# A gated mix of linear attention and a gated MLP on one core: attention's banks copied out whole and stored by rows, its products placed later, one chunk of an operand asked for later

## The chip, the cores and the metric

The kernel runs on one core of one Trainium2 chip. The metric is the device time of one execution in microseconds. The core has five engines that run side by side: PE (matrix products, TensorE), DVE (VectorE), ACT (ScalarE), POOL (GpSimd) and SP (SyncE). In this kernel SP issues the loads and POOL the stores; both go to the same 16 DMA engines.

## The reference

For 2048 tokens of 1024 values, a linear attention with 32 heads and learned feature maps, and a gated MLP, are mixed by a gate per token:

```python
g = sigmoid((x * gate_w).sum(-1, keepdims=True))
q, k, v = split(x @ wqkv)                                  # 32 heads of 32
phi_q = concat(softmax(q @ w_phi), softmax(-(q @ w_phi)))  # phi_k likewise
kv, z = phi_k^T v, sum(phi_k)
a = concat_heads((phi_q kv) / (phi_q z + 1e-6)) @ wo
b = (gelu(x @ w_gate) * (x @ w_up)) @ w_down               # 1024 -> 3584 -> 1024
out = g * a + (1 - g) * b
```

## The kernel before, in words

**Products.** Each large product is split in two by rows, columns and depth, and is made of seven half-size products of sums in place of eight (Strassen's scheme). Each factor is written as a high and a low part in the type fp32r (`high`, a copy on ACT at line 56; `low`, a subtraction on DVE at line 59), and three passes, high by high, high by low and low by high, make one product: 12 matmuls of 128x512 for a depth of 512.

**Units.** The first stage runs over 80 units, in four groups: values, keys, and the two halves of the tokens with queries, gate and up columns. The change from one group to the next is called a change; the third is the one to the last group. A unit has seven slots, in each of which PE makes one of the seven products: a<-x10, p<-s1, c<-x01 (of the unit before), a<-s2, a<-s4 (of the unit before), c11<-x11, b<-s3. The names a, b, c, c11 and p are PSUM banks; x10, s1, s2, x11, s3, s4 and x01 are the seven sums of the token side, each with parts h and l, each read in four chunks of 512. Operands of the weight side live in `wgu`, `tyz` (three buffers) and `v`. At a change the seven token-side sums are loaded anew in chunks to a home, and split; PLANS lists for each change which sum is asked for at which slot and where (line 515). For the last change the home "g" has three places, so the fourth chunk of s4 waits until the first has been split, is then loaded to its place (line 535), and is waited for by `change_parts` (lines 520 to 538).

**Work beside PE.** What ACT, DVE and SP do in a slot is decided while the program is built: each piece of work is a generator that yields the slot from which it may go, the slot by which it must, and its cost on DVE and on ACT, and `run_slot` puts those that fit into the slot. A list called `fillers` holds small products that are put between two of the seven; an entry gives the time from which it may stand. The scheduler knows no loads and no stores: what an engine waits for on the chip is not in its costs. Each engine then runs its own instructions strictly in the order that was written.

**Attention.** In the last group 32 jobs of attention run beside the units. A job loads queries, forms exponentials on ACT (line 1127), normalizes on DVE (1150 to 1173), transposes (1181), splits into high and low (`split_weights`, on lines 56 and 59 into `pts`), and lets PE make four matmuls of 128x512 into two banks called `misc` (line 1198, `attend`). `both` (line 1183) takes the two banks out: the product's halves stand crosswise in the two banks, and their sum is stored to `la` in HBM by a store and an accumulating store. The hidden tiles `h` (three buffers, in turn) hold what goes to HBM: two per job, and those of the units with up columns (DVE lines 760, `less`, and 707), which are stored to `lm`. `h<-b` on line 760 is DVE's subtraction at a unit's start, behind which ACT copies b into c (line 779), into which PE's c<-x01 adds two products later.

**Opening.** Units 1 and 2 also carry out what prepares the first sums; a table called `extra` lists it by slot. `step(1)` is the last of four subtractions (line 149) of raw tiles that stand in `tyz`'s buffers.

**The last stage** multiplies the stored `la` and `lm` by `wo` and `w_down` (line 1462) and adds into the result.

Of the kernel before, what the change touches and what calls it, by code (L numbers as in the profile page):

```python
# [10 lines left out]
AF = mybir.ActivationFunctionType  # L11
OP = mybir.AluOpType
# [21 lines left out]
def tile_gated_mix(ctx: ExitStack, tc: tile.TileContext, x, xT, wkT, wqT, wv, w_phi, wo,  # L34
                   w_gate, w_up, w_down, gate_w, out):
    nc = tc.nc
# [18 lines left out]
    def high(dst, src):  # L55
        nc.scalar.activation(dst, src, AF.Copy)  # L56

    def low(dst, src, dst_h):
        nc.vector.tensor_tensor(dst, src, dst_h.bitcast(F32), OP.subtract)  # L59
# [17 lines left out]
    def hidden():  # L77
        return fa.tile([P, BLK], F32, tag="h", name="h", bufs=3)
# [3 lines left out]
    def x_part(i, part, dtype=F32R):  # L82
        pool = ring if i % 3 == 0 else xa if i < 3 else fa
        return pool.tile([P, KC // 2, BLK], dtype, name=X_NAMES[i] + "hl"[part], bufs=1)
# [24 lines left out]
    left_att = [[dram.tile([2, 2, P, 2, BLK], F32, name=f"la{h}{d}") for d in range(N_ATT)] for h in range(2)]  # L109
# [21 lines left out]
    def spill(h, dst, j, m, **how):  # L131

        nc.gpsimd.dma_start(dst[m // 4][j, m % 2, :, m // 2 % 2, :], h, **how)  # L133
# [52 lines left out]
    with tc.manual_schedule(engines={PE, DVE, ACT, SP}):  # L186
# [30 lines left out]
        for s in range(KC):  # L217
            kc, i = kcs[s], s // 2
# [25 lines left out]
        for s in range(KC):  # L244
            kc, i = kcs[s], s // 2
# [14 lines left out]
            for n, (a, e) in enumerate(PASSES):  # L260
                for blk in (1, 0):
                    for f in range(2):
                        nc.tensor.matmul(plain_banks[blk, f], wide_w[a][:, kc, f * P:(f + 1) * P], xq[blk][e],
                                         start=s == 0 and n == 0, stop=s == KC - 1 and n == 2)
# [25 lines left out]
        def sum_parts(k, q):  # L290
            src, *dst = [t[:, 2 * q:2 * q + 2] for t in (whole[SUM_AT[k]], *x_ops[0, (1, 2, 4, 5)[k]])]
            return (lambda: high(dst[0], src)), (lambda: low(dst[1], src, dst[0]))
# [17 lines left out]
        def sums_high(k, *qs):  # L310
            if x_ops[0, (1, 2, 4, 5)[k]][0] is None:
                x_ops[0, 5] = [x_part(5, part) for part in range(2)]
            for q in qs:
                sum_parts(k, q)[0]()

        def sums_low(k, *qs):
            for q in qs:
                sum_parts(k, q)[1]()
# [14 lines left out]
        streams, fillers, now = [], [], [0]  # L333
        clock, tensor = [0.0, 0.0], [0.0]

        def start(gen, ready=0.0):
            streams.append([next(gen), len(streams), gen, ready])
# [50 lines left out]
        passed = [0.0]  # L388
# [73 lines left out]
        def change_half(t, half):  # L462

            yield t - 13, NEVER, 0.0
            while keys_left[0]:
                yield now[0] + 1, NEVER, 0.0
            if half == 1:
                plain = lambda j, k: wk_fold[j][4 * k:4 * k + 4].rearrange("k p n -> p k n")
                s4 = k_sum
            else:  # L470
                plain = lambda j, k: xT3[:, 4 * k:4 * k + 4, (2 * HALF[half] + j) * BLK:(2 * HALF[half] + j + 1) * BLK]
                s4 = x_sum[HALF[half]]
            srcs = [plain(1, 0), s4[0], s4[1], plain(1, 1), s4[2], s4[3], plain(0, 1)]
            homes = {}
            for i, at, home in PLANS[half]:
                yield t + at, t + at, 0.0
                while home in busy or half == 2 and (gating[0] if home in ("w", "y") else folding[0]):
                    yield now[0] + 1, now[0] + 1, 0.0
                if isinstance(home, int):
                    x = x_part(home, 1, F32)  # L480
                    x = [x[:, j] for j in range(KC // 2)]
                else:
                    if home not in homes:
                        homes[home] = home_parts(half, home)
                    x = homes[home]
                busy[home] = KC // 2
                for j in range(len(x)):
                    nc.sync.dma_start(x[j], srcs[i][:, j])
                need = t + (min(NEED[i], NEED[home] - 1) if isinstance(home, int) else NEED[i])
                start(change_parts(half, i, home, x, t, need, srcs[i]))  # L490
# [6 lines left out]
        def home_parts(half, home):  # L497
# [10 lines left out]
            if home == "y":  # L508
# [5 lines left out]
        held_homes, gating = [], [True]  # L514
        PLANS = {1: ((0, -9, "x"), (1, -8, "w"), (2, -5, "x"), (3, -4, "w"), (4, -1, "x"), (6, 1, "w"), (5, 3, "x")),
                 2: ((0, -9, "w"), (1, -8, "y"), (2, -5, "w"), (3, -5, "x"), (4, -4, "y"), (6, 0, "w"), (5, 3, "x")),
                 3: ((0, -7, "x"), (1, -5, "y"), (2, -4, "x"), (3, -3, "z"), (4, -1, 3), (5, 0, "g"), (6, 3, "z"))}

        def change_parts(half, i, home, raw, t, need, src):

            yield max(now[0] + 3, t + LAST[i] + 1), need - 3, 0.0
            while i in busy:
                yield now[0] + 1, now[0] + 1, 0.0
            x_ops[half, i] = [x_part(i, part) for part in range(2)]
            for j in range(KC // 2):
                h = x_ops[half, i][0][:, j]
                if j == 3 and raw[3] is raw[0]:
                    yield now[0] + 3, need - 2, 0.0
                yield now[0], need - 3, 0.0, 0.63
                high(h, raw[j])  # L530
                low_j = low_part(x_ops[half, i][1][:, j], raw[j], h, need, home, j)
                if len(raw) == 3 and not j:
                    yield from low_j
                    raw = [*raw, raw[0]]
                    nc.sync.dma_start(raw[3], src[:, 3])
                else:
                    start(low_j, passed[0])

        def low_part(dst, x, h, need, home, j):

            yield now[0], need - 2, 0.69
            low(dst, x, h)
            busy[home] -= 1
            if not busy[home]:
                del busy[home]
                if home == "z":
                    for k in held_homes:
                        held[k] = False
# [558 lines left out]
        def attention(jobs):  # L1107
# [4 lines left out]
            while job:  # L1112
                half, g, j = job
# [21 lines left out]
                z = shared["z"]  # L1135
# [47 lines left out]
                def both(po, half=half, g=g, j=j):  # L1183
                    yield now[0] + 1, now[0] + 3, 0.0, 1.2
                    hs = [hidden() for _ in range(2)]
                    for i, (a, b) in enumerate(((0, 64), (64, 0))):
                        nc.scalar.activation(hs[i][:64], po[0][a:a + 64], AF.Copy)
                        nc.scalar.activation(hs[i][64:], po[1][b:b + 64], AF.Copy)
                        if i == 0:
                            yield now[0], now[0] + 2, 0.0, 1.2  # L1190
                    spill(hs[0], left_att[half], j, g)
                    spill(hs[1], left_att[half], j, g, accum_op=OP.add)

                def attend(kbs=kbs, pts=pts, both=both):
                    po = [misc(), misc()]
                    for q in range(2):
                        for p in range(2):
                            nc.tensor.matmul(po[p], kbs[:, p].rearrange("p i a b -> p (i a b)"), pts[:, q, p, :],  # L1198
                                             start=q == 0, stop=q == 1)
                    free[0] = True  # L1200
                    start(both(po))

                def push(attend=attend):
                    yield now[0], NEVER, 0.0
                    fillers.append((passed[0], attend, 4, range(1, 7)))

                def split_weights(pts=pts, push=push):
                    yield now[0], NEVER, 0.0, 1.05
                    high(pts[:, 0], f2)
                    yield now[0], NEVER, 1.25  # L1210
                    low(pts[:, 1], f2, pts[:, 0])
                    lows[0] = True
                    start(push())

                start(split_weights(), passed[0])
            while not free[0]:
                yield now[0] + 1, NEVER, 0.0
# [45 lines left out]
        def step(q):  # L1263
            return (lambda: next(x_sums[q])), 1.22
# [4 lines left out]
                    outs[1], (lambda: sums_high(1, 0, 1), 0.0, 2.1), (lambda: sums_low(1, 0, 1), 2.44)],  # L1269
                2: [*folds[2:4], (lambda: sums_high(2, 0, 1), 0.0, 2.1), (lambda: sums_low(2, 0, 1), 2.44), step(0)],  # L1270
                4: [*folds[4:], outs[2], outs[3]]},
            2: {2: [step(1), (lambda: sums_high(3, 0), 0.0, 1.05)],
                3: [(lambda: sums_low(3, 0), 1.22), (lambda: sums_high(3, 1), 0.0, 1.05), (lambda: sums_low(3, 1), 1.22), *puts[:1]],
                5: puts[1:2]},
            3: {1: puts[2:3], 2: puts[3:]}}
        for n, u in enumerate(units):
# [10 lines left out]
    po = [ctx.enter_context(tc.tile_pool(name=f"po{n}", bufs=b, space=PSUM, reuse_waits="tile"))  # L1287
          for n, b in enumerate((3, 3, 1, 1))]
    fours = [[po[n]] * 3 + [po[n + 2]] for n in range(2)]
    with tc.tile_pool(name="op", bufs=1, reuse_waits="tile") as op, tc.manual_schedule(engines={PE, DVE, ACT, SP}):  # L1290
# [142 lines left out]
        for s, (turn, d, k) in enumerate(steps):  # L1433
# [26 lines left out]
            for m, c in order:  # L1460
                for n, (a, e) in enumerate(PASSES):
                    nc.tensor.matmul(ps[c], lefts[s][:, a, m, c * P:(c + 1) * P], made[k][:, e, m],  # L1462
                                     start=d == 0 and m == 0 and n == 0, stop=d == n_duo - 1 and m == 1 and n == 2)
# [40 lines left out]
```

## Time and profile before

| what | us |
|---|---|
| median of three runs (2322.46, 2326.59, 2326.56) | 2326.56 |
| the profiled execution | 2325.13 |
| its span, first to last instruction | 2323.2 |
| PE busy | 2310.4 |
| DVE, ACT, POOL busy | 1746.4, 1206.0, 389.4 |

The span is what the profile's views are about; 1.9 us lie around it. The view of waits says for each engine what it was idle for. In a timeline a row has its start, its duration, the engine, the line, what it writes and reads, how many instructions it merges, and in brackets the idle time before it with what ended it. A matmul's own duration is longer than the distance to the next, since matmuls overlap. `w` is the name of both work tiles.

### The profile page before, as it was taken

How to read it: one execution, taken by the hardware profiler on the slowest of the kernel's cores; microseconds unless marked ns; L12 is line 12 of the kernel's file. 1: busy time of each engine (PE TensorE's matmuls, PEld its weight loads, DVE VectorE, ACT ScalarE, POOL GpSimd, SP SyncE). 2: the span in 40 equal slices, each digit the busy share in tenths (PEclk: the TensorE clock that was granted, in tenths of full speed). 3: DMA queues.
4: the chain of work that ended last, by engine and by line, in shares of the span. 5: the costliest groups of instructions: out<-in, count | busy, mean ns of one | idle time of the engine just before them, and what ended most of it. 6: DMA issues, size and time to landing. Idle time of an engine off the chain costs nothing. (4 is left out here: it accounts for less than half of the span.)

```text
span 2323.2 us, 29698 instructions
## 1 busy us (share of the span) xinstructions
PE 2310.4 (99%) x10414; PEld 1918.5 (83%) x10414; DVE 1746.4 (75%) x2390; ACT 1206.0 (52%) x1691; POOL 389.4 (17%) x620
## 2 busy tenths in 40 slices
PE   9999999999999999999999999999999999999999
PEld 8888888888888888878887888788888888888887
DVE  8677567788888888867888888884774868867874
ACT  6555456565656565546687777775533322323221
POOL 2443322222222222221111111111000000000000
PEclk9999999999999999999999999999999999999999
DMA  7899989888889999997888887787874867977873
GB/s 234 293 324 326 310 301 348 293 310 291 311 298 304 328 311 324 305 319 258 259 261 251 263 255 257 238 258 234 313 245 149 289 236 264 339 253 274 295 262 134
DMA packets 264981, 645.44 MB, mean 278 GB/s; under 512 B 32208, under 2 KB 68576, under 8 KB 256896
## 3 DMA queue, kind: packets, MB, share of 16 engines
q1 hardware_dynamic: 205888, 428.67, 55.3%
q0 software_dynamic: 58672, 214.74, 26.5%
q8 instruction: 82, 1.34, 0.2%
q14 instruction: 67, 0.55, 0.1%
q10 hardware_dynamic: 272, 0.13, 0.0%
HBM read 429.00 MB, written 214.70 MB: 277 GB/s over the span
## 5 line engine op out<-in xcount | busy, mean ns | idle before, releaser
L1462 PE MATMUL po<-tw,wgu 128*128 128x512 f32 x1344 | 309.8, 389 | 0.0
L56 ACT ACTIVATE wgu<-stage 128x1024 fp32r<-128x1024 f32 (+2 forms) x166 | 172.6, 1040 | 255.1 <-DVE stage L1352 159.0
L1462 PEld LDWEIGHTS po<-tw,wgu 128*128 128x128 f32 x1344 | 252.3, 188 | 52.4
L59 DVE TENSOR_TENSOR wgu<-stage,wgu 128x1024 fp32r<-128x1024 f32 (+2 forms) x135 | 161.6, 1197 | 86.8 <-ACT wgu L56 85.8
L747 PE MATMUL a<-s4h,v 128*128 128x512 f32 x632 | 209.1, 392 | 0.0
L747 PE MATMUL c<-x01h,tyz 128*128 128x512 f32 x624 | 205.8, 391 | 1.2 <-ACT c L779 1.2
L747 PE MATMUL p<-s1h,tyz 128*128 128x512 f32 x624 | 205.0, 389 | 1.4 <-ACT w L765 1.4
L747 PE MATMUL a<-s2h,tyz 128*128 128x512 f32 x624 | 205.4, 390 | 0.7 <-DVE tyz L59 0.5
L747 PE MATMUL b<-s3h,tyz 128*128 128x512 f32 x624 | 205.6, 390 | 0.3 <-ACT b L796 0.3
L747 PE MATMUL a<-x10h,wgu 128*128 128x512 f32 x624 | 205.3, 390 | 0.0
L747 PE MATMUL c<-x11h,wgu 128*128 128x512 f32 x624 | 205.0, 389 | 0.0
L1462 PE MATMUL po<-tw,wl 128*128 128x512 f32 x672 | 156.9, 389 | 0.0
L1462 PE MATMUL po<-tyz,wgu 128*128 128x512 f32 x672 | 155.2, 389 | 0.0
L1462 PEld LDWEIGHTS po<-tw,wl 128*128 128x128 f32 x672 | 126.1, 188 | 26.2
L1462 PEld LDWEIGHTS po<-tyz,wgu 128*128 128x128 f32 x672 | 126.1, 188 | 26.2
L747 PEld LDWEIGHTS a<-s4h,v 128*128 128x128 f32 x632 | 119.3, 189 | 24.8
L747 PEld LDWEIGHTS p<-s1h,tyz 128*128 128x128 f32 x624 | 117.1, 188 | 26.7 <-ACT w L765 2.2
L747 PEld LDWEIGHTS c<-x01h,tyz 128*128 128x128 f32 x624 | 117.2, 188 | 25.9 <-ACT c L779 2.1
L747 PEld LDWEIGHTS a<-s2h,tyz 128*128 128x128 f32 x624 | 117.0, 188 | 25.7 <-DVE tyz L59 1.0
L747 PEld LDWEIGHTS b<-s3h,tyz 128*128 128x128 f32 x624 | 117.2, 188 | 24.6 <-ACT b L796 0.7
L747 PEld LDWEIGHTS c<-x11h,wgu 128*128 128x128 f32 x624 | 117.1, 188 | 24.3
L747 PEld LDWEIGHTS a<-x10h,wgu 128*128 128x128 f32 x624 | 117.1, 188 | 24.1
(448 smaller groups left out, 4870.6 us busy)
## 6 DMA issues: line engine op xcount, KB each, us to landing
stage<-lm SPq DMA_DIRECT2D x98, 512.0 KB, 4.4
sr<-in_w_down SPq DMA_DIRECT2D x84, 512.0 KB, 4.9
sl<-lm SPq DMA_DIRECT2D x70, 512.0 KB, 4.7
lm<-h POOLq DMA_DIRECT2D x112, 256.0 KB, 5.2
stage<-in_w_gate SPq DMA_DIRECT2D x42, 512.0 KB, 5.6
stage<-in_w_up SPq DMA_DIRECT2D x42, 512.0 KB, 7.0
vs<-vt SPq DMA_DIRECT2D x32, 512.0 KB, 4.1
la<-h POOLq DMA_DIRECT2D x64, 256.0 KB, 5.0
```

The source lines that it names most:

```text
L56: nc.scalar.activation(dst, src, AF.Copy)
L59: nc.vector.tensor_tensor(dst, src, dst_h.bitcast(F32), OP.subtract)
L747: nc.tensor.matmul(dst, w[:, h, kc, :], xq[e][:, kc, :], start=first and kc == 0 and i == 0, stop=kc == 3 and i == 2, skip_group_check=True)
L1462: nc.tensor.matmul(ps[c], lefts[s][:, a, m, c * P:(c + 1) * P], made[k][:, e, m], start=d == 0 and m == 0 and n == 0, stop=d == n_duo - 1 ...
```

## The change

It has four parts.

1. `both` copies each of the two banks out whole (two ACT copies of 128x512 in place of four of 64x512), and stores by rows: of each tile one half of the rows goes to its place by a plain store, the other half to the other tile's place by an accumulating one, four DMAs of 64x512 in place of two of 128x512. The sums are the same.
2. The attention products may stand 0.8 us later in `fillers`, and the generator that pushes them starts behind the low part of `pts`.
3. At the third change s1 is asked for one slot earlier, and the wait for a fourth chunk is two slots longer and is due one slot later.
4. `step(1)` moves from slot 2 of unit 2 to slot 0.

```diff
-                 3: ((0, -7, "x"), (1, -5, "y"), (2, -4, "x"), (3, -3, "z"), (4, -1, 3), (5, 0, "g"), (6, 3, "z"))}
+                 3: ((0, -7, "x"), (1, -6, "y"), (2, -4, "x"), (3, -3, "z"), (4, -1, 3), (5, 0, "g"), (6, 3, "z"))}
...
                 if j == 3 and raw[3] is raw[0]:
-                    yield now[0] + 3, need - 2, 0.0
+                    yield now[0] + 5, need - 1, 0.0
...
                     hs = [hidden() for _ in range(2)]
-                    for i, (a, b) in enumerate(((0, 64), (64, 0))):
-                        nc.scalar.activation(hs[i][:64], po[0][a:a + 64], AF.Copy)
-                        nc.scalar.activation(hs[i][64:], po[1][b:b + 64], AF.Copy)
-                        if i == 0:
-                            yield now[0], now[0] + 2, 0.0, 1.2
-                    spill(hs[0], left_att[half], j, g)
-                    spill(hs[1], left_att[half], j, g, accum_op=OP.add)
+                    for h, bank in zip(hs, po):
+                        nc.scalar.activation(h, bank, AF.Copy)
+                    dst = left_att[half][g // 4][j, g % 2, :, g // 2 % 2, :]
+                    for i in range(2):
+                        for p in range(2):
+                            nc.gpsimd.dma_start(dst[64 * p:64 * p + 64], hs[p][64 * i:64 * i + 64],
+                                                **(dict(accum_op=OP.add) if i else {}))
...
-                    fillers.append((passed[0], attend, 4, range(1, 7)))
+                    fillers.append((passed[0] + 0.8, attend, 4, range(1, 7)))
...
-                    start(push())
+                    start(push(), passed[0])
...
-            2: {2: [step(1), (lambda: sums_high(3, 0), 0.0, 1.05)],
+            2: {0: [step(1)], 2: [(lambda: sums_high(3, 0), 0.0, 1.05)],
```

On DVE in unit 2 the subtraction of raw tiles (L149) changes places with what follows the copy of b; a piece of the difference, with what goes and what comes:

```order
 L167 TENSOR_TENSOR vh<-c_85,vh 128x4x64 x2
 L760 TENSOR_TENSOR h<-b,w_535 128x512
+L149 TENSOR_TENSOR raw<-raw 128x1024
 L167 TENSOR_TENSOR w_535<-h,w_535 128x4x64 x2
 L59 TENSOR_TENSOR v<-o_646,v 128x512
-L149 TENSOR_TENSOR raw<-raw 128x1024
 L59 TENSOR_TENSOR tyz<-stage,tyz 128x1024
 L59 TENSOR_TENSOR s4l<-raw,s4h 128x1024 x2
```

The subtraction stands two rows, three instructions, earlier.

On ACT behind the third change, in the unit whose s4 is the first of the new half, the order before was (`x01h` and `s4h` are token-side sums, `pts` the exponentials that the sums of keys and values read at line 995):

```order
L56 ACTIVATE x01h<-stage 128x512 x4
L714 ACTIVATE h<-c_85 128x512
L765 ACTIVATE w_535<-p 128x512
L779 ACTIVATE c<-b 128x512
L794 ACTIVATE c_85<-a 128x512
L56 ACTIVATE s4h<-w_535 128x512
L56 ACTIVATE pts<-w_557 128x1024
L56 ACTIVATE wgu<-stage 128x1024
```

and it is now:

```order
L56 ACTIVATE x01h<-stage 128x512 x4
L714 ACTIVATE h<-c_85 128x512
L765 ACTIVATE w_535<-p 128x512
L779 ACTIVATE c<-b 128x512
L794 ACTIVATE c_85<-a 128x512
L56 ACTIVATE pts<-w_557 128x1024
L56 ACTIVATE wgu<-stage 128x1024
L714 ACTIVATE h<-c 128x512
L56 ACTIVATE s4h<-w_535 128x512
```

The fourth chunk of s4 moved behind `pts` and two more copies; on DVE its low part moved behind the low part of `pts` too. The first pass over z and the normalization (lines 1046 and 971) moved from ahead of the s4 chunks to just ahead of `pts`.

On POOL, where an attention job's stores stand among those of a unit with up columns, the order before was (the numbers name the tiles in the order in which they are asked for; of four `h` tiles that follow each other the fourth takes the first one's buffer):

```order
L133 DMA la00_94<-h_11987 128x512
L133 DMA la00_94<-h_12108 128x512
L133 DMA lm04_102<-h_12132 128x512
L133 DMA la00_94<-h_12109 128x512
L133 DMA lm04_102<-h_12147 128x512
```

and at a like place it is now:

```order
L1191 DMA la10_96<-h_9703 64x512
L1191 DMA la10_96<-h_9704 64x512
L133 DMA lm01_99<-h_9729 128x512
L1191 DMA la10_96<-h_9703 64x512
L1191 DMA la10_96<-h_9704 64x512
L133 DMA lm01_99<-h_9740 128x512
```

Before, the first tile (12108) was read by one store, ahead of the accumulating one; now the first tile (9703) is read by a plain store and by an accumulating one, and the latter waits for the former to have landed. The fourth tiles, 12147 and 9740, are h<-b of line 760.

## The prediction

> **What bounds the kernel now.** I read the page's first lines first, then the view of waits for PE alone, then the timeline at the longest of them. The page says that PE is what counts:
>
> ```profile
> span 2323.2 us, 29698 instructions
> PE 2310.4 (99%) x10414; PEld 1918.5 (83%) x10414; DVE 1746.4 (75%) x2390; ACT 1206.0 (52%) x1691; POOL 389.4 (17%) x620
> ```
>
> PE is idle for 12.8 us in all, and the change leaves PE's 10414 matmuls as they are. So nothing it does to ACT, DVE, POOL or the DMA queues counts unless it shortens or makes a stop of PE. These are the stops (engine and line, what ended the wait: us in total, times, longest):
>
> ```profile
> PE misc L995 <- DVE pts L59: 3.2, 1, 3.2
> PE p L747 <- ACT w L765: 1.4, 2, 1.0
> PE c L747 <- ACT c L779: 1.2, 2, 1.0
> PE misc L1198 <- DVE pts L59: 1.2, 3, 0.5
> ...
> PE a L747 <- DVE tyz L59: 0.5, 1, 0.5
> PE b L747 <- ACT b L796: 0.3, 1, 0.3
> PE a L747 <- ACT tyz L56: 0.2, 1, 0.2
> ```
>
> The rest of the idle time is the start and the end of the program. A product's pace is one row of the chain, 12 matmuls in 2.73 us, 0.227 us each:
>
> ```profile
> 1480.62 2.73 PE a L747 x12
> ```
>
> **The change part by part.** *The step of the sums moved from slot 2 to slot 0 of unit 2.* DVE's and ACT's timelines, then PE's:
>
> ```profile
> 50.38 0.76 DVE L167 TENSOR_TENSOR w<-h,w 128x256 fp32r<-128x256 f32 x2 [2.47 <-ACT w L164]
> ...
> 51.66 1.22 DVE L149 TENSOR_TENSOR raw<-raw 128x1024 f32<-128x1024 f32 x1
> ```
>
> ```profile
> 50.56 0.58 ACT L794 ACTIVATE c<-a 128x512 f32<-128x512 f32 x1
> 52.91 1.06 ACT L56 ACTIVATE tyz<-stage 128x1024 fp32r<-128x1024 f32 x1 [1.77 <-DVE raw L149]
> ```
>
> ```profile
> 53.46 0.39 PE L747 MATMUL c<-x01h,wgu 128*128 128x512 f32 x1
> 54.02 0.50 PE L747 MATMUL a<-s2h,tyz 128*128 128x512 f32 x1 [0.17 <-ACT tyz L56]
> ...
> 55.28 0.73 PE L747 MATMUL a<-s2h,tyz 128*128 128x512 f32 x2 [0.53 <-DVE tyz L59]
> ```
>
> ACT's copy into `tyz` waits for DVE's L149, which reads the last raw tile of that buffer. L149 now stands ahead of the 0.76 us pair, in the 2.47 us in which DVE is idle: it ends before 50.4 instead of at 52.9. ACT then starts `tyz` behind L794, at 51.1 instead of 52.91, and DVE's low part follows from 52.2 to 53.4, ahead of PE's 53.69. Both stops go. The first matmul came 0.33 us late (54.02 against 53.46 + 0.23) and the third 0.69 us, and after each stop the next one is 0.11 us slower (0.50 long instead of 0.39): **-1.25 us**. Next late there is the low part of s4, which moves up with it. The cover is that idle time; without it the gain is nothing.
>
> *The third change's fourth chunk asked for later.* PE's timeline and the window's granted clock (the 0.65), then ACT's and DVE's timelines:
>
> ```profile
> 1007.54 0.39 PE L747 MATMUL a<-s2h,tyz 128*128 128x512 f32 x1
> 1011.08 1.19 PE L995 MATMUL misc<-pts,vs 128*128 128x256 f32 x8 [3.15 <-DVE pts L59]
> 1012.11 0.40 PE L747 MATMUL a<-s4h,v 128*128 128x512 f32 x1
> ...
> 1016.22 0.40 PE L747 MATMUL a<-s4h,v 128*128 128x512 f32 x1
> ```
>
> ```profile
> 1011.08:1016.00 4.92, 4.92 (x19) 4.05 (x20) 3.58 (x4) 1.63 (x3) 0.00 (x0) 0.65 0.78 276
> ```
>
> ```profile
> 1006.39 0.63 ACT L56 ACTIVATE s4h<-w 128x512 fp32r<-128x512 f32 x1 [5.39 <-DMA w<-xs]
> 1006.93 1.04 ACT L56 ACTIVATE pts<-w 128x1024 fp32r<-128x1024 f32 x1
> ```
>
> ```profile
> 1007.06 0.69 DVE L59 TENSOR_TENSOR s4l<-w,s4h 128x512 fp32r<-128x512 f32 x1 [5.96 <-ACT s4h L56]
> 1007.67 0.71 DVE L1046 TRANSPOSE_TENSOR_REDUCE rim<-w 128x16 f32<-128x512 f32 x1
> ...
> 1008.53 0.67 DVE L956 TENSOR_REDUCE extremes<-kx 128x16 f32<-128x512 f32 x1
> ...
> 1009.72 1.21 DVE L59 TENSOR_TENSOR pts<-w,pts 128x1024 fp32r<-128x1024 f32 x1
> ```
>
> ACT stood 5.39 us for the fourth chunk's load, and `pts` behind it; PE waited 3.15 us for `pts`, and the clock was then granted at half for a while. In the new order `pts` stands ahead of s4's fourth chunk on both engines. DVE is free at 1001.1 (1007.06 less its 5.96 of idle time). L1046 takes 0.71, L971 1.2 (a pass over 1024, as L149 above), so ACT's high part, 1.04, runs from 1003.0 to 1004.1 beside L956 and L957 (0.67 each, to 1004.4); the low part, 1.21, ends at 1005.6, 2.2 us ahead of PE's 1007.77. The fourth chunk is still copied at about 1006.4 and split by 1007.7; PE needs it only three quarters into a<-s4, behind L995's 1.03 and 9 matmuls, at 1010.8. So the stop goes: 3.31 us of late start, and the 11 matmuls from 1012.11 to 1016.22 took 4.11 us where 2.49 is the pace, 1.62 us: **-4.93 us**. On SP the second zs load (L1044) now waits for L1046 until about 1001.8, and the `tq0y` and `tq1y` loads stand behind it. PE takes those two and four products behind L995, at 1014 and 1019, so that the 12 us up to there cover them; uncovered they would be a stop of their own. The vs load, the s1 chunk asked for a slot earlier and the sums of kv (L1027 to L1033) move within idle time; no stop of PE names them.
>
> *Banks copied whole, products placed 0.8 us later.* Per attention job ACT makes two copies of 128x512 in place of four of 64x512. L794 above (128x512, 0.58) and L1187 below (64x512, 0.57) cost the same: 2 x 0.58 x 32 jobs, 37 us less on an engine that is 52% busy. No stop is as long as that helps, but the seven small ones behind 1040 (c twice, misc L1198 three times, p's 0.4, b) come from ACT or DVE being late by 0.5 us or so: 3.1 us idle, and 0.27 each for the late restart (at 1473.25 below the idle time is 1.03, the start 1.19 late, the next 0.11 slower), 5.0 us. The 0.8 us covers the three of L1198 (longest 0.5). Between nothing and 5.0 I take **-4.0**, since a new order leaves one or two of its own. POOL issues 64 more DMAs, at most 0.89 us each (the row of `la` below) in the 536 us of the jobs, and it is 17% busy: nothing by itself.
>
> *Stored by rows: what it adds.* Before, the first `h` tile of a job was read by one plain store, the second by the accumulating one. Now both are read by a plain store of half the rows and an accumulating one, and the accumulating store waits on POOL for the plain one to land; queued behind it there is the other accumulating store and the next `lm` store. So the first `h` tile is held for two landings in place of one. Who waits is DVE's L760 h<-b, three `h` tiles on. Four times in this trace it already waits for a plain store; the view of waits, and one case in ACT's, POOL's, DVE's and PE's timelines:
>
> ```profile
> DVE h L760 <- DMA la<-h: 15.2, 4, 4.9
> ```
>
> ```profile
> 1463.99 0.57 ACT L1187 ACTIVATE h<-misc 64x512 f32<-64x512 f32 x1
> ```
>
> ```profile
> 1465.48 0.56 POOL L133 DMA_DIRECT2D la<-h  x1 [7.67 <-ACT h L1188]
> ...
> 1472.29 0.88 POOL L133 DMA_DIRECT2D la<-h  x1 [5.57 <-DMA la<-h]
> ```
>
> ```profile
> 1471.89 0.69 DVE L760 TENSOR_TENSOR h<-b,w 128x512 f32<-128x512 f32 x1 [4.88 <-DMA la<-h]
> ```
>
> ```profile
> 1466.62 0.39 PE L747 MATMUL a<-x10h,wgu 128*128 128x512 f32 x1
> ...
> 1473.25 0.50 PE L747 MATMUL c<-x01h,tyz 128*128 128x512 f32 x1 [1.03 <-ACT c L779]
> ```
>
> The unit's first matmul is at 1466.62, and its c<-x01 is due two products later, 1472.06. From h<-b to c<-x01 it is 1.36 us (1471.89 to 1473.25), so DVE may start h<-b up to 4.1 us into a unit for nothing; later costs PE as much. The `h` tile was held 7.9 us here (1463.99 to 1471.89). How long it will be held: copy 0.58, to POOL 0.3, a landing, 0.5 to the accumulating issue, a landing, 0.1 to DVE. No store of 64 rows of 2 KB is in the trace; the nearest are `la` with 128 rows and L1036's `kz` with 64 small ones (POOL's rows, and the last line of each answer):
>
> ```profile
> L133 POOL DMA_DIRECT2D la<-h x64: 539/708/890, 1069.3 to 1605.4; - x64
> ...
> DMA to landing us min/median/max: 2.3/5.2/8.4
> ```
>
> ```profile
> L1036 POOL DMA_DIRECT2D kz<-h x32: 613/828/1382, 417.3 to 1026.3; - x32
> ...
> DMA to landing us min/median/max: 1.8/4.3/7.3
> ```
>
> At 4.3 a landing it is 10.1 us, at 5.2 11.9, at the shortest 2.3 6.1. I take 4.3, nearest in partitions. Counting matmuls in the changed program's order, the copy whose tile h<-b takes next stands 15 matmuls ahead of the unit at two places, 25 at two, 28 at one, 39 or more at the others. At 0.227 us, and 0.3 late as in the case above (13 matmuls, 2.63 us), 15 is 3.1 us: 10.1 - 3.1 - 4.1 = 2.9, with the restart 3.2, twice 6.4. 25 is 5.4 us: 0.6, with restart 0.9, twice 1.8. 28 is nothing. **+8.2 us**.
>
> Sum: -1.25 - 4.93 - 4.0 + 8.2 = -2.0. The profiled execution took 2325.13 us (its span and 1.9 around it): **2323.2**. The median of the three runs, 2326.56, is 1.4 above that execution, the lowest, 2322.46, 2.7 below; the forecast lies within 0.2% (4.65 us, about what a measurement of this kernel can tell from no change) of the median either way.
>
> **The rivals.** *The tiles come free in time (B).* With landings near 2.3 us, the shortest row of `la`, the hold is 6.1 us, under the 7.2 that 15 matmuls allow. No new stop, and the small ones go nearly all: -11.2, 2314 to 2315. Against it stand the medians of 4.3 and 5.2 while SP's loads run; for it, that half the bytes go at a time. The Trainium skill, "DMA: Bandwidth & Descriptors", section "Anatomy of one DMA — SWDGE (gpsimd) path", has 2.0 us and bytes over 436e3 for such a DMA; that is an estimate of 2.3 us for 128 KB, and by that rule this rival's time. The trace agrees with it at the shortest `la` landing (2.3), not at the median.
>
> *The hold becomes the bound: slower (C).* The place is DVE's L760 h<-b at those five places. Break-even is a hold of 10.6 us (0.5 more at four places gives the 2.0 back). At landings of 4.8, between the rows, it is 11.1: 3.9 us idle at the two near places, over the 3.15 us behind which the clock fell, so 3.9 + 0.27 + 1.6, twice 11.5; 1.9 twice at 25; 1.2 at 28: +16.4, net +6.2, 2331.3. At 5.2 it is 2335. For it: the held `h` already cost 4.9 us on DVE once. Against: half the bytes. The skill's "TensorE: Matmul & The Clock Gate", section "What's actually happening", has the clock halved after an idle window of 3413 ns that runs free; a 3.9 us stop need not cover a whole one, and without the two halvings this rival would be 2328. The trace's 3.15 us was enough once.
>
> *The fourth chunk's stop doesn't go, or comes back at another wait (D).* L971 now stands behind L1046, which needs a zs load, and SP holds there; if that is over 2.2 us late, PE stops at L995 again. Then the 4.93 is missing: 2328.1.
>
> **How the numbers follow.** The forecast (A) 0.45, with 2319 to 2327 as its own range, of which 0.12 lies below 2321.9; B 0.22, all faster; C 0.20, of which 0.17 above 2331.2; D 0.13, of which 0.03. Faster 0.34, same 0.46, slower 0.20. The range, from B's time to most of C's, is 2315 to 2331.5.
>
> **What would show it.** The rows at 54 and 55 us are without idle time if the first step is right. L995's row near 1008 has no bracket, and no window near it is below 1.00 clock. In the waits, "PE misc L1198 <- DVE pts" is gone or under 0.5; "DVE h L760 <- DMA la<-h" grows from 15.2 us to 25 or more with single waits of 6 us or more, and "PE c L747 <- ACT c L779" grows from 1.2 to 6 or 7. If `la` lands within 3 us, B holds; if c<-x01 waits over 10 us in all or the clock falls behind it, C. What would make the whole wrong: a new stop behind ACT's or DVE's changed order that none of these rows shows.

## The result, and the profile after

The changed kernel takes 2342.87 us (median of 6 runs, 2340.88 to 2344.91); the kernel before took 2325.9 (6 runs). The ratio is 1.0077, 95% interval 1.0064 to 1.0090: 17 us slower, outside the range. The profiled execution took 2344.91 us, its span is 2343.1. Of four executions of one kernel below, the one with the third change undone, one took 3907.86 us at a granted clock of 0.556; the median given there is of the other three. The page's first lines:

```profile
span 2343.1 us, 29735 instructions
...
PE 2315.8 (99%) x10414; PEld 1920.3 (82%) x10414; DVE 1746.8 (75%) x2390; ACT 1169.5 (50%) x1631; POOL 434.8 (19%) x684
```

ACT lost 36.5 us of work, as worked out. The span grew by 19.9 us all the same, with as many matmuls, so PE stops more. The view of waits for PE (engine and line, what ended the wait: us in total, times, longest):

```profile
PE misc L1198 <- DVE pts L59: 10.7, 6, 3.3
PE c L747 <- ACT c L779: 7.5, 3, 3.3
PE p L747 <- ACT w L765: 3.7, 4, 2.3
...
PE a L747 <- ACT c L794: 0.4, 1, 0.4
```

L995's wait is gone. The waits of L1198 grew from 1.2 to 10.7 us and those of c from 1.2 to 7.5. The same view for DVE says what stands behind both:

```profile
DVE h L760 <- DMA la<-h: 34.1, 8, 6.1
...
DVE h L760 <- DMA lm<-h: 11.9, 4, 4.8
```

The first of them was 15.2 us in four waits before. One of the eight cases in the timelines of ACT, POOL, DVE and PE (start, us, engine, line, operation, idle time ahead of it and what ended it):

```profile
1216.80 1.08 ACT L1187 ACTIVATE h<-misc 128x512 f32<-128x512 f32 x2
```

```profile
1217.69 1.09 POOL L1191 DMA_DIRECT2D la<-h  x2 [9.94 <-ACT h L1187]
1221.51 1.72 POOL L1191 DMA_DIRECT2D la<-h  x2 [2.74 <-DMA la<-h]
```

```profile
1229.29 0.69 DVE L760 TENSOR_TENSOR h<-b,w 128x512 f32<-128x512 f32 x1 [5.58 <-DMA la<-h]
1230.02 0.69 DVE L707 TENSOR_TENSOR h<-h,w 128x512 f32<-128x512 f32 x1
1230.63 1.22 DVE L59 TENSOR_TENSOR pts<-w,pts 128x1024 fp32r<-128x1024 f32 x1
```

```profile
1228.51 0.61 PE L1198 MATMUL misc<-pts,kbs 128*128 128x512 f32 x2
1231.90 0.74 PE L1198 MATMUL misc<-pts,kbs 128*128 128x512 f32 x2 [2.78 <-DVE pts L59]
```

The first `h` tile is written at 1216.80. Its plain store is issued at 1217.69. The accumulating one can be issued at 1221.51, when the plain one has landed, and DVE gets the tile at 1229.29: 12.5 us, of which the accumulating store, from its issue to DVE's start, takes 7.8. DVE stands 5.58 us with the low part of `pts` queued behind it, and PE stops for `pts`, not for c<-x01: here the job's products stand between p and c.

Such stops can be added up: for each pair of neighbouring matmuls, the time from start to start less 0.227 us, where that is more than 0.1 us, the half-clock ones included. From 9 us on, past the program's start, this gives 12.4 us before and 31.9 after, a difference of 19.5 for 19.9 of span. Of the 31.9, seven stops behind a held tile make 22.6: 1105.7 (1.25), 1231.9 (3.05), 1248.2 (1.75), 1318.1 (3.53), 1361.2 (2.70), 1486.2 (5.13) and 1572.1 (5.14). One near the third change makes 4.17:

```profile
996.51 1.40 ACT L56 ACTIVATE x01h<-stage 128x512 fp32r<-128x512 f32 x2 [2.03 <-DMA stage<-in_xT]
998.10 0.63 ACT L56 ACTIVATE x01h<-stage 128x512 fp32r<-128x512 f32 x1 [0.19 <-DMA stage<-in_xT]
999.51 0.63 ACT L56 ACTIVATE x01h<-stage 128x512 fp32r<-128x512 f32 x1 [0.78 <-DMA stage<-in_xT]
...
1000.52 0.59 ACT L765 ACTIVATE w<-p 128x512 f32<-128x512 f32 x1
```

```profile
1001.16 0.50 PE L747 MATMUL p<-s1h,tyz 128*128 128x512 f32 x1 [2.34 <-ACT w L765]
```

ACT waits for the loads of x01, and the copy that empties p's bank (L765) stands behind these four copies; before, L765 ran at 998.58. PE, 0.95 us further on than before at this place, waits 2.34 us for it, and the clock falls to half. The load of the product's other operand, `tq0y`, landed at 1000.69, so PE would have stood some 2 us without L765 too. SP's timeline shows what is new ahead of these loads:

```profile
987.40 0.38 SPq L927 DMA_DIRECT2D vs<-vt  x1
988.73 4.01 SPq L488 DMA_DIRECT2D stage<-in_xT  x4
992.80 0.60 SPq L678 DMA_DIRECT2D tyz<-tq0y  x1
```

Before, the `vs` load was issued at 976.65, and x01's four loads (`stage<-in_xT`) landed from 993.94 to 997.54; now `vs` stands just ahead of them, and they land from 996.48 to 999.48. That `vs` alone makes them late was not tested.

### The profile page after: what moved, and what is told of

It reads as the page before. It is cut to its first block, busy times and chain, and to the rows that moved or that the text cites. A ratio compares the mean times of both kernels' runs of the same rounds, so it can differ in the third digit from the quotient of the medians.

```text
span 2343.1 us, 29735 instructions
## 1 busy us (share of the span) xinstructions
PE 2315.8 (99%) x10414; PEld 1920.3 (82%) x10414; DVE 1746.8 (75%) x2390; ACT 1169.5 (50%) x1631; POOL 434.8 (19%) x684
## 4 chain that ended last, share of the span: by engine, by line
PE 72%; issue 15%; DMA 6%; POOL 4%; DVE 2%; ACT 1%; SPq 0%; POOLq 0%; DVEq 0%; ACTq 0%
PE po L1462 29%; PE a L747 17%; PE c L747 11%; PE p L747 6%; PE b L747 5%; DMA la<-h 3%; POOL la L1191 2%; PE misc L995 1%; POOL lm L133 1%; DMA lm<-h 1%; PE c L263 0%; DMA qx<-q 0%; DMA wq<-fold 0%; PE misc L422 0%; DMA wx<-xs 0%
## 5 line engine op out<-in xcount | busy, mean ns | idle before, releaser
L56 ACT ACTIVATE wgu<-stage 128x1024 fp32r<-128x1024 f32 (+2 forms) x166 | 172.6, 1040 | 254.3 <-DVE stage L1352 161.1
L1191 POOL DMA_DIRECT2D la<-h x128 | 90.2, 733 | 305.7 <-ACT h L1187 203.6
```

What stands on the lines that cost most here:

```text
L1191: nc.gpsimd.dma_start(dst[64 * p:64 * p + 64], hs[p][64 * i:64 * i + 64], **(dict(accum_op=OP.add) if i else {}))
```

## The experiments

Times are medians; each ratio is against runs of the kernel before on the same chip. Their medians were 2326.07 us (beside the old stores put back, the second halves aside, the third change undone, and the old stores with the old third change), 2327.24 (the new stores alone, the two halves of the third change, and the tiles stored whole), 2325.70 (the last two kernels) and 2325.74 (the rest).

**The old stores put back.** In the changed kernel, `both` becomes the one of before:

```
-                    for h, bank in zip(hs, po):
-                        nc.scalar.activation(h, bank, AF.Copy)
...
+                        nc.scalar.activation(hs[i][:64], po[0][a:a + 64], AF.Copy)
+                        nc.scalar.activation(hs[i][64:], po[1][b:b + 64], AF.Copy)
...
+                    spill(hs[0], left_att[half], j, g)
+                    spill(hs[1], left_att[half], j, g, accum_op=OP.add)
```

> The changed kernel with the old copies and stores of an attention job (four copies of half a bank, one plain store of 128 rows from the first h tile, one accumulating from the second); the other edits stay. Theory H (the h tile held for two landings): the PE stops of the changed kernel that stand behind DVE's L760 h<-b or h<-a waiting for la<-h are those at 1105.7, 1231.9, 1248.2, 1318.1, 1361.2, 1486.2 and 1572.1 us, 22.5 us of lateness with what the half clock costs; they go, and 'DVE h L760 <- DMA la<-h' falls from 34.1 to under 16 us: 2319 to 2324. Rival O (the products placed 0.8 us later and the low part's push moved, which make pts late): the stops at L1198 and c<-x01 stay, the time is over 2335.

Measured: 2321.71 us, ratio 0.9985 (0.9975 to 0.9994). The three edits that are left make the kernel a little faster than before; the new copies and stores cost 21.2 us. The waits for DVE and PE:

```profile
DVE h L760 <- DMA la<-h: 9.8, 4, 4.1
```

```profile
PE p L747 <- ACT w L765: 1.8, 2, 1.4
PE misc L191 <- DVE ones L188: 1.1, 1, 1.1
PE a L747 <- DVE h L760: 0.9, 1, 0.9
PE misc L1198 <- DVE pts L59: 0.9, 2, 0.6
PE c L747 <- ACT c L779: 0.6, 1, 0.6
```

**The second halves stored aside.** Whole-bank copies and four stores of 64 rows as in the changed kernel, but the two that accumulate become plain stores to another buffer. The second half of each bank is left out of the result.

```
-                            nc.gpsimd.dma_start(dst[64 * p:64 * p + 64], hs[p][64 * i:64 * i + 64],
-                                                **(dict(accum_op=OP.add) if i else {}))
+                            nc.gpsimd.dma_start((aside if i else dst)[64 * p:64 * p + 64], hs[p][64 * i:64 * i + 64])
```

> The changed kernel with the accumulating stores replaced by plain ones of the same rows into a DRAM buffer of their own, so that no store waits for another and the second half of each bank is not added to the result. As many stores, as many bytes, the same copies. Theory H: an h tile is held for one landing, 6 to 7 us, which the places allow: the stops go as without the new stores, 2319 to 2325, and the wait of DVE for la<-h falls under 10 us. Rival R (the row stores themselves are slow, or 64 more of them crowd POOL and the DMA engines): the time stays over 2335.

Measured: 2318.65, ratio 0.9972 (0.9963 to 0.9982). As many stores and as many bytes, 24 us less than the changed kernel: it is neither the copies, nor POOL's issues, nor stores of 64 rows. What is left is the accumulating store, which waits for the plain one and lands later itself, while the tile is held. The time is also 3 us below that with the old copies and stores; whether the whole-bank copies are worth that was not tested by itself. DVE's waits for these stores:

```profile
DVE h L761 <- DMA ls<-h: 11.8, 4, 4.8
```

They were to fall under 10 us and are at 11.8; no PE stop above 0.8 us stands behind them.

**Only the first tile freed early.** The first tile's second half goes aside (and is left out of the result); the second tile keeps its accumulating store.

```
+                            nc.gpsimd.dma_start((dst if i == 0 or p else aside)[64 * p:64 * p + 64], hs[p][64 * i:64 * i + 64],
+                                                **(dict(accum_op=OP.add) if i and p else {}))
```

> The changed kernel with only the first h tile of a job freed after one landing: its second half is stored aside by a plain store and not added; the second tile still has its accumulating store. As many stores and bytes. Theory H as the prediction put it (the first tile is the one that DVE's h<-b takes next): the stops go, 2318 to 2323. Rival T (either tile does the harm, or the wait of POOL for the landing, behind which the lm stores queue): 2330 or more.

Measured: 2318.51, ratio 0.9971 (0.9959 to 0.9982). POOL still waits for landings here, and it does no harm:

```profile
POOL la L1192: 107.3, 32
```

(who waited for an `la` store: line, us, times; in the changed kernel it is 101.9 us in 43). So it is the first tile's hold and not POOL's wait.

**The new stores alone.** The kernel before with the changed `both`, all else as before:

```
-                    spill(hs[0], left_att[half], j, g)
-                    spill(hs[1], left_att[half], j, g, accum_op=OP.add)
...
+                            nc.gpsimd.dma_start(dst[64 * p:64 * p + 64], hs[p][64 * i:64 * i + 64],
+                                                **(dict(accum_op=OP.add) if i else {}))
```

> The kernel before with the new copies and stores alone (two whole-bank copies, four stores of 64 rows, two of them accumulating); sums, third change and placing as before. Theory H (the hold of two landings does the whole harm): the time rises by about what undoing these stores took off the changed kernel, 21.2 us: 2340 to 2350. Rival I (it harms only together with the products placed 0.8 us later, which brings the copy nearer to the next unit): 2326 to 2333.

Measured: 2347.03, ratio 1.0089 (1.0074 to 1.0104). The harm needs no other edit. Not every stop there is the first tile's hold: two, of 0.9 and 2.4 us near 1235 and 1494, stand behind an `lm` store that DVE's h<-b waits for.

**The third change undone.** In the changed kernel:

```
-                 3: ((0, -7, "x"), (1, -6, "y"), ...
+                 3: ((0, -7, "x"), (1, -5, "y"), ...
...
-                    yield now[0] + 5, need - 1, 0.0
+                    yield now[0] + 3, need - 2, 0.0
```

> The changed kernel with the third change as before (s1 at slot -5, the fourth chunk asked for as before); the other edits stay. In the changed kernel the stop at L995 near 1011 us (4.89 us with the half clock) was gone, but p<-s1 at 1001.2 us stopped for 4.17 us. Theory S (one stop took the other's place, and both come from that edit's order): L995 stops again for 4 to 5 us, the stop at 1001 goes, and the time is 2342 to 2345, the same. Rival N (the stop at 1001 has nothing to do with the edit): both stops are there, 2347 or more. Rival G: neither, 2338.

Measured: 2341.55, ratio 1.0078 (1.0061 to 1.0095): no difference from the changed kernel. In its trace L995 stops for 4.71 us with the half clock, and p<-s1 near 999 for 0.18. One stop took the other's place.

**Old stores and old third change.** The kernel before with the sums in slot 0 and the later placing alone:

```
-            2: {2: [step(1), (lambda: sums_high(3, 0), 0.0, 1.05)],
+            2: {0: [step(1)], 2: [(lambda: sums_high(3, 0), 0.0, 1.05)],
...
-                    fillers.append((passed[0], attend, 4, range(1, 7)))
+                    fillers.append((passed[0] + 0.8, attend, 4, range(1, 7)))
...
-                    start(push())
+                    start(push(), passed[0])
```

> The kernel before with two of the edits alone: the step of the sums in slot 0, and the products placed 0.8 us later with the low part's push moved. By the stops of before: 1.25 us less in unit 2, and of the three L1198 stops (0.47, 0.81, 0.70) all or most: 2322 to 2324 against 2325.9. Rival O (the later placing makes stops of its own): 2327 or more.

Measured: 2322.64, ratio 0.9989 (0.9979 to 0.9998). L995 stops here for 5.06 us with the half clock. With the third change, in the first run above, L995 does not stop and p<-s1 stops for 1.64 us; the medians are only 0.9 us apart, the executions of that kernel reaching from 2318.0 to 2322.8.

**The two halves of the third change, each alone, with the old stores.** Against the run with the old stores, first the one line and then the other goes back:

```
-                    yield now[0] + 5, need - 1, 0.0
+                    yield now[0] + 3, need - 2, 0.0
```

```
-                 3: ((0, -7, "x"), (1, -6, "y"), ...
+                 3: ((0, -7, "x"), (1, -5, "y"), ...
```

> The kernel with the old stores, of the third change only the s1 chunk at slot -6; the fourth chunk is asked for as before. Theory P (the stop of p<-s1 at 999 to 1001 us, 1.2 to 4.2 us in the runs with the whole edit, comes from the loads that this moves): that stop is there with over 1 us, and L995's of 4.7 to 5.1 us near 1010 as well: 2323 to 2326. Rival Q (it comes from the fourth chunk's load and copy): no stop near 1000 above 0.6 us, 2322.6 as without the edit.

> The kernel with the old stores, of the third change only the fourth chunk asked for later; s1 stays at slot -5. Theory P: L995's stop near 1010 goes and p<-s1 at 999 us stops for 0.2 to 0.6 us as without the edit: 2317 to 2320, below the 2321.7 with the whole edit. Rival Q: p<-s1 stops for over 1 us: 2321 to 2323.

Measured: 2320.91, ratio 0.9978 (0.9968 to 0.9988), with s1 moved; 2320.68, ratio 0.9972 (0.9962 to 0.9981), with the fourth chunk later. Neither theory held as put. Either half by itself takes L995's long stop away (none, and 0.82 us), and in both p<-s1 stops near 1000 us (1.25 and 1.53). So that stop is not one half's doing. The traces show two ways in which L995's stop goes. With s1 moved, SP issues the fourth chunk's load (L535) ahead of the second zs load (L1044). First the run before these two, then the one with s1 moved:

```profile
993.59 0.65 SPq L1044 DMA_DIRECT2D w<-zs  x1
994.75 0.33 SPq L535 DMA_DIRECT2D w<-xs  x1
```

```profile
994.00 0.61 SPq L535 DMA_DIRECT2D w<-xs  x1
...
1001.82 0.32 SPq L1044 DMA_DIRECT2D w<-zs  x1
```

The chunk lands at 1001.51 instead of 1005.64, and ACT, which copies it ahead of `pts`, is no longer held. With the chunk asked for later it lands as late as ever, at 1007.0, but `pts` stands ahead of its copy. The stop of p<-s1 differs too: where s1 moved it ends with the `tq0y` load, where the chunk is later with L765.

**The placing undone.** Old stores, sums in slot 0, the third change; 0.8 and the push's start as before.

```
-                    fillers.append((passed[0] + 0.8, attend, 4, range(1, 7)))
+                    fillers.append((passed[0], attend, 4, range(1, 7)))
...
-                    start(push(), passed[0])
+                    start(push())
```

> The kernel with the old stores, the sums in slot 0 and the third change, but the products placed as before (no 0.8, the low part's push as before). Theory: the 0.8 covers small stops behind 1040 us, 5.0 us in the kernel before, 3.0 us with the 0.8 and the old stores (2321.7): 2322 to 2325. Rival: the placing is worth nothing by itself, 2320 to 2322.

Measured: 2327.7, ratio 1.0009 (1.0000 to 1.0018), 6.0 us over the same kernel with the 0.8 (2321.71, beside other runs of the kernel before). Its stops behind 1040 us add up to 12.0 us, many at L1198 and c; with the 0.8 it is 3.0. That is above the ranges of both theories: the placing is worth more than forecast.

**Ways to add the halves without holding a tile.** The first stores each tile whole, by one DMA to two places, and adds the second place to the first by a DMA from DRAM to DRAM:

```
+                    pair = att_pair[half][g // 4][:, j, g % 2, :, g // 2 % 2, :]
+                    for p in range(2):
+                        nc.gpsimd.dma_start(pair[:, 64 * p:64 * p + 64], hs[p])
...
+                        nc.gpsimd.dma_start(t[0], t[1], accum_op=OP.add)
```

> The changed kernel with another way to add the two halves of a bank: each h tile is stored whole by one plain store into two DRAM places, and the second place is added to the first one job later by an accumulating DMA from DRAM to DRAM, for which no h tile is held. Theory H: an h tile is held for one landing as where the halves were not added (2318.65 there): 2316 to 2322, no DVE wait for la<-h above 5 us. Rival R (the DRAM-to-DRAM sum blocks POOL or slows the loads): 2326 or more.

Measured: 2415.57, ratio 1.0384 (1.0365 to 1.0404), a miss for two reasons. The sum was not issued a job later as meant, but at once. And the stores were slow. The view of DMAs (from, to, KB each, median us to landing), and POOL's timeline at the first job:

```profile
la<-h POOLq DMA_DIRECT2D x64, 256.0 KB, 12.1
la<-la POOLq DMA_DIRECT2D x32, 256.0 KB, 6.2
```

```profile
1072.09 1.66 POOL L1192 DMA_DIRECT2D la<-h  x2
1087.54 0.89 POOL L1196 DMA_DIRECT2D la<-la  x1 [13.80 <-issue]
```

12.1 us for a store of 256 KB; the same tile as one block of 128 rows took 4.9 with the old stores. The first store landed after 12.4 us, with no sum under way, so it is not the sums that slow it. One landing of 12 us holds a tile as long as two of 6.

The next keeps the four plain stores of 64 rows and issues the sum (128 rows, DRAM to DRAM) behind the next job's stores; a second one has the fourth chunk alone of the third change besides.

```
+                    att_sums.append((dst, aside))
...
+                        d, t = att_sums.pop(0)
+                        nc.gpsimd.dma_start(d, t, accum_op=OP.add)
```

> The changed kernel with the second halves stored aside by plain stores, as in the run that held each h tile for one landing (2318.65 us), and added by one accumulating DMA of 128 rows from DRAM to DRAM, issued behind the next job's stores, where its source has long landed. The whole result is computed. Theory H: h tiles are held for one landing, 2317 to 2321, DVE's wait for la<-h under 6 us. Rival R (a DRAM-to-DRAM sum crowds POOL or the DMA engines, whatever waits for it): 2324 or more.

> The same with s1 of the third change back at slot -5, the fourth chunk still asked for later. With the old stores this took 1.0 us off (2321.7 to 2320.7), within what two runs can differ by. Theory: 2316 to 2321, the same as its neighbour within 2 us. Rival: L995's stop of 4.9 us comes back, 2322 to 2326.

Measured: 2323.22, ratio 0.9986 (0.9978 to 0.9995), and 2322.2, ratio 0.9985 (0.9976 to 0.9994): some 20 us less than the changed kernel, but 4.6 and 3.6 us more than the run without sums (2318.65). The second lies in its rival's range, but not for the rival's reason: L995 does not stop in its trace. The last two issue the sum ahead of the next job's stores, for both tiles and for the first tile only:

```
+                    if att_sums:
+                        att_sums.pop()()
...
+                    att_sums.append(lambda: nc.gpsimd.dma_start(dst[:64], aside[:64], accum_op=OP.add))
```

> The run with the late DRAM sum, but each job's sum is issued ahead of the next job's stores, so that POOL does not wait for the stores just issued (there: 132 us of POOL's time in 29 waits for ls<-h, and DVE waited 9.5 us for lm<-h stores queued behind). The whole result is computed. Theory W (that wait of POOL was what cost 4.6 us against the run without sums, 2318.65): POOL's wait for ls<-h falls under 30 us, 2317 to 2321. Rival X (the DRAM sums' own traffic costs it): 2322 to 2325 again.

> Only the first h tile's second half goes aside and is added by a DRAM sum of 64 rows ahead of the next job's stores; the second tile keeps its accumulating store. The whole result is computed. Without the sum this took 2318.51 us. Theory W: 2318 to 2321. Rival X, with half the sums' traffic: 2320 to 2322. Rival T (POOL's wait for the second tile's landing does harm behind the sum): 2324 or more.

Measured: 2321.78, ratio 0.9982 (0.9973 to 0.9991), and 2319.65, ratio 0.9972 (0.9961 to 0.9982). In the first, POOL still waited 137 us for the aside stores:

```profile
POOL la L1196 <- DMA ls<-h: 137.0, 30, 7.3
```

That expectation was ill put: the sum now waits in a time in which POOL has little else to do. The run does not tell whether the sums' traffic costs the 2 to 3 us that are left. The second does what was wanted: the whole result is computed, the first tile is held for one landing, and the time is that of the run without sums (2318.51) within 1.2 us. It and the kernel with the old stores and the fourth chunk alone (2320.68, also 0.9972) have the lowest ratios of those that compute everything, though the intervals of others overlap with theirs.

## Why the prediction was wrong

*What bounds the kernel.* Right: the span moved by what PE's stops moved (19.5 of 19.9 us). Those 19.5 are about -1.0 for the sums, -0.7 at the third change, -1.3 of small stops and +22.6 behind held tiles.

*The sums in slot 0, -1.25.* Right within 0.25. The first `a<-s2` matmuls of unit 2 are now

```profile
53.88 0.39 PE L747 MATMUL a<-s2h,tyz 128*128 128x512 f32 x1
54.10 0.39 PE L747 MATMUL a<-s2l,tyz 128*128 128x512 f32 x1
54.47 0.73 PE L747 MATMUL a<-s2h,tyz 128*128 128x512 f32 x2
```

with no idle time, and the third 0.14 us late.

*The third change, -4.93.* The mechanism at L995 was right, the sum was not. What failed is "The vs load, the s1 chunk asked for a slot earlier and the sums of kv (L1027 to L1033) move within idle time; no stop of PE names them"; the prediction did not look at p<-s1. The `vs` load did move, by 10.8 us, to just ahead of x01's loads, and L765 and the `tq0y` load came behind those. That is rival D, "comes back at another wait", three products ahead of L995, where D had looked for it. In the changed kernel 4.89 us went and 4.17 came; with the old stores the edit is worth about 1 us.

*The small stops, -4.0.* In kind right, in size half: behind 1040 us such stops were 4.9 us before, and with the old stores 3.0 are left. Without the 0.8 they are 12.0, so that most of what the placing covers are stops that the other edits' new order brings.

Without the stores, then, the forecast was -1.25 - 4.93 - 4.0 = -10.2, and the run with the old stores gave -4.4 by the medians: 6 us too much hope, nearly all of it on the third change and on the small stops.

*Stored by rows, +8.2.* This is the term that failed: 22.6 us. The mechanism is the one put forward, the first tile held for two landings, and the runs with a tile freed early show it. Its size was wrong in four ways.

- The distances were counted "in the changed program's order", one matmul after another at 0.227 us. That has the copy 39 or more matmuls ahead of the unit, about 9 us, at three of the places. On the chip ACT comes to it later. At the case shown above the unit begins at 1223.07 and the copy at 1216.80, 6.3 us ahead; from the job's products (1211.28 to 1212.35) to the copy ACT has this to do:

```profile
1210.04 1.28 ACT L1127 ACT_TABLE_LOAD   x1
1211.33 1.27 ACT L1127 ACTIVATE w<-stage 64x512 f32<-64x512 f32 x2
1212.63 1.06 ACT L56 ACTIVATE wgu<-stage 128x1024 fp32r<-128x1024 f32 x1
1213.72 1.27 ACT L1127 ACTIVATE w<-stage 64x512 f32<-64x512 f32 x2
1215.01 1.28 ACT L702 ACT_TABLE_LOAD   x1
1216.30 0.60 ACT L702 ACTIVATE w<-c 128x512 f32<-128x512 f32 x1
```

  So the three places that were to cost nothing (1231.9, 1361.2 and 1486.2) cost 10.9 us, and the two with 25 matmuls (1318.1 and 1572.1), whose copies came 3.1 and 3.3 us ahead instead of 5.4, cost 8.7 instead of 1.8. The two others, with 28 matmuls (1105.7) and at an h<-a (1248.2), were to be free and cost 3.0.
- "At 4.3 a landing": the two landings were to take 8.6 us. Over the 32 jobs the plain stores landed in 3.6 us at the median, 2.2 at the shortest, and the accumulating ones in 5.5, up to 9.2. At five places (1231.9, 1318.1, 1361.2, 1486.2 and 1572.1) the first tile's two took 9.9 to 11.5 us together, and the hold was 11.2 to 13.0, not 10.1. It was not always the accumulating one: at 1318.1 and 1572.1 the plain store took 6.6 and 6.8, the accumulating one 3.4 and 3.2. Rival B's 2.3, the shortest landing of a store of 256 KB before, was near the shortest of the new stores of 128 KB, but at none of these places.
- The price was that of c<-x01 alone, "later costs PE as much". At three of the five the job's products stand between p and c, and the low part of `pts` (1.22 us) is queued on DVE behind h<-b, so PE stops earlier than at c.
- Behind two of the stops, with 3.3 us of idle time each, the clock was granted at half for 3.4 us, 1.6 us more each time.

The other way round, the two places with 15 matmuls, which were to cost 6.4 us, cost 0.5 at c<-x01, and 1.3 at the attention products 8 us on, whose `pts` DVE reaches late from the same wait. There h<-b waits for an `lm` store (4.84 us the longest), and in the program's waits it names one store alone. The rule that the fourth tile asked for takes the first one's buffer does not hold there.

Rival C was this case: "The hold becomes the bound", with the hold just over its break-even at a landing of 4.8 us. It had the mechanism and the sign, and gave 2331.3; the range ended there. Most of its price stood at the two places that turned out nearly free.

Of the signs put forward, DVE's waits for `la` (34.1 us, the longest 6.1) and those of c (7.5) came. That of L1198 did not: it was to be gone or under 0.5 us and is the largest, 10.7; and the clock, which was to stay whole near L995, fell at 1002.24.

## What to carry to other kernels

Before a store is split into a plain and an accumulating one, ask how long the source tile is then held, and which waiting instruction takes its buffer next: with two landings in series it was 10.1 to 13.0 us at the seven places here. Distances between engines are to be read from the trace's times, not counted in the program's order, where an engine with its own backlog lies between. And an edit that takes one stop away moves the next one into sight: each product of the same unit wants its own due time worked out.

## What the runs showed of the hardware

*The clock falls before a whole window is idle.* The half-clock stretches of one execution begin on a grid of 3.413 us, whatever PE does: at 1002.24, 1486.93 and 1572.26 in the changed kernel, 142.0 and 25.0 such steps apart. The view of windows (PE, weight loads, DVE, ACT and POOL busy, then the granted clock, DMA share, GB/s) behind a stop of 3.26 us and behind one of 3.25:

```profile
1486.93:1490.34 3.41, 3.41 (x10) 2.66 (x9) 3.38 (x6) 3.34 (x8) 0.00 (x0) 0.50 0.32 114
1318.11:1321.50 3.39, 3.39 (x15) 2.81 (x16) 1.22 (x3) 3.35 (x5) 0.56 (x1) 1.00 0.51 198
```

Stops of one length, and only the first was followed by half the clock. It filled 80% of one step of the grid; the other lay across two, 41% and 54%. The stop of 2.34 us at 1001.16 filled 68% of a step and was followed by half the clock. Over all the runs but the one with the sum issued at once, the twelve steps that were more than 56% idle were all followed by it, and none under 52%; between the two both occur. In the run left out, three steps of 59 to 79% were not followed by it; each was itself at half the clock. The Trainium skill, "TensorE: Matmul & The Clock Gate", section "What's actually happening", has a free-running window of 3413 ns, which the grid confirms, and the clock lowered after at least one idle window; here a window a little over half idle was enough.

*A store to two blocks landed later.* One DMA of 128 rows to one block landed in 4.9 us at the median (old stores), to two blocks of 64 rows in 12.1. The Trainium skill, "DMA: Bandwidth & Descriptors", section "Why a DMA increments its semaphore by 16 and not by 1", says that the slowest dimension that is not 1 sets how many of the 16 engines a DMA uses; for the second store's destination that dimension is 2. The trace agrees in which of the two is slower; the engines were not counted. The slower stores differ in one thing more: the trace has 448 packets of 8 bytes for each of the 64, and such packets are in no other trace here. So the cause stays open.
